# Closing an expert's first token group after four batches, and sending list entries one at a time

## The chip, the core and the metric

The kernel runs on one core of a Trainium2 chip. A core has five engines that run side by side: PE (TensorE, matmuls and transposes), DVE (VectorE), ACT (ScalarE), POOL (GpSimd) and SP (SyncE, which here only issues DMAs). They wait for each other through semaphores; each runs its own instructions strictly in order. The metric is the device time of one execution in microseconds (us), lower is better.

## The reference

```python
def reference(...):                        # B=8 batches, H=8 heads, 512 local + 32 global rows, D=64
    s_g  = scale * q_g @ concat(k_g, k_l).T            # global rows see everything
    out_g = softmax(s_g) @ concat(v_g, v_l)
    s_l  = concat(scale * q_l @ k_g.T, banded(scale * q_l @ k_l.T))   # |i - j| <= 32
    out_l = softmax(s_l) @ concat(v_g, v_l)
    x = rows of concat(out_g, out_l): 8 * 544 = 4352 tokens, 512 features
    do_compute = x @ w_skip > 0                        # tokens that go through an expert
    e_idx = argmax(x @ w_gate); gate_w = softmax(x @ w_gate)[e_idx]
    out = x;  out[do] += gate_w * (relu(x[do] @ w1[e_idx]) @ w2[e_idx])   # 8 experts, F = 1024
```

## The kernel before

**Attention** runs in 32 *units*, one for each pair of heads of a batch (`u` is the unit, `b = u // 4` the batch). The loop body is a list of step names, `ORDER`, which is walked once per unit; `cur`, `prev` and `old` are the pairs of units u, u-1 and u-2, so two more turns of the loop (u = 32 and 33, with `NU` = 32) drain the pipeline. Every engine gets its instructions in the order in which these steps issue them. Steps of weight here: `probs` (DVE, ACT: masked scores and exponentials), `scale 0` and `scale 1` (POOL, L435, multiply by the inverse sums), `scale_g` (POOL, L468), `turn` (PE, L476, transposes of the scaled probabilities), `turn_pg` (PE, L492), `turned` (DVE and ACT, L483, copies out of PSUM), `values` (PE, L530/L539), `leave` (ACT and DVE, L560). `rows` and `late_rows` turn a finished batch back to rows and write them to `out`.

**Routing.** When a batch's (or a pair of batches') rows are done, `route` returns some twenty small steps that find each token's expert and its place in that expert's list. They go into the list `stages`; each `seam` in `ORDER` (seven per unit) calls `tick`, which pops one (two from u = 28 on). `counts` (PE, L644 to L650) sums over tokens and needs `ohb` from DVE or POOL. The result `slu` holds list addresses, and one `send` per 128 tokens then writes (token, weight) entries into the DRAM list `lst` with an indirect DMA from POOL (L688). Batches go in the groups (0,1), (2,3), (4,5), 6, 7 with 8, 9, 8, 4 and 5 sends. Up to unit 28 the step `sends` issues two at the end of a unit, in units 29 and 30 up to four; in unit 30 one more goes at each of four seams, and batch 6's four go at the end of unit 31.

**First expert.** Its first group of 256 list places has to be complete before the others are. So `base[:, 0]` is raised to at least 256 after batch 5, `slots` (SP) loads the group's entries from `lst` at the end of unit 30, and in unit 31 `index` (DVE, L102) and `gather` (POOL, two indirect DMAs, L119) fetch its tokens into `xfirst`. `turn_x` (PE, L206) transposes them in turn 32.

**Experts.** Then eight experts are computed one after the other, each with a group of 256 tokens, and those with more tokens with a second group. Sends that remain (batch 7's) go out in `lists()` during the first expert, whose second group and the next expert's first one are gathered after that.

Line numbers in profile rows are those of this kernel.

## Time and profile before

| what | value |
|---|---|
| time of three runs | 475.98 us median (472.29, 475.98, 480.51) |
| the profiled execution | 477.54 us, of which 475.8 us are the span from the first to the last instruction |
| mean granted TensorE clock | 0.981 of full speed |
| PE busy | 444.5 us, 93% of the span |
| DVE, ACT, POOL busy | 302.9, 282.7 and 231.5 us |

The attention part ends and the first expert's matmuls begin at about 229 us. A row of the timeline gives start, duration, engine, line, operation and tiles; the bracket at its end is the engine's idle time just before it and who ended that.

### The profile page before, as it was taken

What the parts mean: (1) busy time and instruction counts of PE and PEld (TensorE: products, weight loads), DVE (VectorE), ACT (ScalarE), POOL (GpSimd) and SP (SyncE); (2) the same over time, 40 slices, a digit from 0 to 9 for tenths busy, and PEclk for the clock granted to TensorE, in tenths of its full rate; (3) what the DMA queues carried; (4) which work ended last, traced back from release to release, by engine and by line L of the source; (5) the groups of instructions that cost most, each with busy time, mean ns of one, the idle gap of its engine ahead of it and who ended that gap; (6) DMA issues with size and microseconds to landing.
All of it is one profiled execution on the core that took longest, in us unless ns stands there. A gap on an engine that the chain in (4) does not pass through costs nothing. (4 is left out here: it accounts for less than half of the span.)

```text
span 475.8 us, 13573 instructions
## 1 busy us (share of the span) xinstructions
PE 444.5 (93%) x4962; PEld 376.2 (79%) x4962; DVE 302.9 (64%) x1207; ACT 282.7 (59%) x867; POOL 231.5 (49%) x240
## 2 busy tenths in 40 slices
PE   7899999998899998878998999998999999999995
PEld 3677878777687777666987989997978989789894
DVE  7898888986778978573563248573823838239351
ACT  5599999998889987753432135452613636137240
POOL 7567777779866768856355032413101432004111
PEclk9799999999999999979998999999999999999999
DMA  8999898989999797401627019392820949308200
GB/s 253 288 324 314 284 326 302 299 297 234 296 269 279 191 290 228 135 2 46 201 23 286 38 50 326 118 338 70 309 102 7 302 154 318 124 21 287 79 2 34
DMA packets 50595, 93.34 MB, mean 196 GB/s; under 512 B 15644, under 2 KB 19996, under 8 KB 50496
## 3 DMA queue, kind: packets, MB, share of 16 engines
q1 hardware_dynamic: 44096, 79.73, 52.2%
q0 software_dynamic: 6400, 12.35, 7.7%
q8 instruction: 56, 0.92, 0.8%
q14 instruction: 43, 0.35, 0.3%
HBM read 82.91 MB, written 14.67 MB: 205 GB/s over the span
## 5 line engine op out<-in xcount | busy, mean ns | idle before, releaser
L398 ACT ACTIVATE prob<-prob,nmx 128x160 f32<-128x160 f32 x256 | 106.8, 424 | 17.9 <-DVE nmx L393 15.4
L435 POOL TENSOR_TENSOR prob<-prob,inv 128x640 f32<-128x640 f32 x64 | 80.7, 1262 | 37.9 <-DVE inv L431 23.6
L932 ACT ACTIVATE hh<-ph 128x256 fp32r<-128x256 f32 x72 | 27.8, 387 | 76.1 <-PE ph L926 73.7
L1014 POOL DMA_INDIRECT out_dram<-yo,six x12 | 12.2, 1019 | 118.1 <-DVE yo L1013 108.8
L945 PE MATMUL py<-w2h,hh 128*128 128x512 f32 x144 | 57.7, 401 | 1.2 <-issue 1.2
L380 PE MATMUL pss<-ks,qs 64*64 64x160 f32 x1024 | 55.4, 315 | 2.6 <-issue 1.4
L945 PE MATMUL py<-w2l,hh 128*128 128x512 f32 x144 | 56.6, 393 | 0.0
L945 PE MATMUL py<-w2h,hlw 128*128 128x512 f32 x144 | 56.5, 392 | 0.0
L539 PEld LDWEIGHTS pv<-ptT,vw 128*64 128x64 f32 x1024 | 43.1, 141 | 12.4 <-issue 11.7
L539 PE MATMUL pv<-ptT,vw 128*64 128x64 f32 (+1 forms) x1024 | 48.6, 241 | 1.9 <-issue 1.9
L398 ACT ACTIVATION_READ_ACCUMULATOR prob<-prob,nmx 128x1 f32 x256 | 49.8, 195 | 0.0
L926 PE MATMUL ph<-xh,w1l 128*128 128x256 f32 x288 | 45.4, 280 | 1.1 <-issue 1.1
L926 PE MATMUL ph<-xh,w1h 128*128 128x256 f32 x288 | 45.5, 280 | 0.7 <-PEq L1103 0.7
L380 PEld LDWEIGHTS pss<-ks,qs 64*64 64x64 f32 x1024 | 36.9, 138 | 11.1 <-issue 7.1
L926 PE MATMUL ph<-xl,w1h 128*128 128x256 f32 x288 | 45.2, 279 | 0.0
L933 DVE SCALAR_TENSOR_TENSOR hlw<-ph,hh 128x256 fp32r<-128x256 f32 x72 | 30.3, 420 | 22.6 <-ACT hh L932 20.7
L688 POOL DMA_INDIRECT lst<-dat,slu x34 | 34.1, 1004 | 14.7 <-issue 6.9
L926 PEld LDWEIGHTS ph<-xh,w1h 128*128 128x128 f32 x288 | 39.2, 189 | 1.7 <-issue 1.1
L926 PEld LDWEIGHTS ph<-xh,w1l 128*128 128x128 f32 x288 | 38.6, 188 | 1.3 <-issue 1.3
L476 PE MATMUL pst<-ident,prob 128*128 128x128 f32 x256 | 39.7, 281 | 0.0
L926 PEld LDWEIGHTS ph<-xl,w1h 128*128 128x128 f32 x288 | 38.8, 189 | 0.0
L213 ACT CAST xh<-xt 128x512 fp32r<-128x512 f32 (+1 forms) x22 | 11.2, 552 | 46.0 <-PE xt L206 46.0
(178 smaller groups left out, 970.8 us busy)
## 6 DMA issues: line engine op xcount, KB each, us to landing
raw<-in_w_dram SPq DMA_DIRECT2D x56, 512.0 KB
vw<-in_v_dram SPq DMA_DIRECT2D x32, 512.0 KB
ks<-in_kT_dram SPq DMA_DIRECT2D x32, 400.0 KB
out_dram<-xr SPq DMA_DIRECT2D x32, 256.0 KB
qs<-in_qT_dram SPq DMA_DIRECT2D x31, 256.0 KB
raw<-in_w_dram POOLq DMA_DIRECT2D x8, 512.0 KB
vgs<-in_vgl_dram SPq DMA_DIRECT2D x32, 64.0 KB
lst<-dat,slu POOLq DMA_INDIRECT x34
```

What stands on the lines that cost most here:

```text
L213: nc.scalar.copy(xh[:, c:c + step, ts_], p3[:, c:c + step])
L380: nc.tensor.matmul(banks[odd][head(h ^ odd), j * W:(j + 1) * W], q[head(h), w * QB:(w + 1) * QB], window(k[head(h)], w), start=True, stop= ...
L398: nc.scalar.activation(pt[:, i, :], pt[:, i, :], AF.Exp, bias=nmx[:, i:i + 1], scale=-1.0, accum_out=sums[:, i, 0:1],)
L435: nc.gpsimd.tensor_mul(pt[:, sl, :], pt[:, sl, :], inv[:, sl].unsqueeze(2).to_broadcast([P, 4, W]),)
L476: nc.tensor.transpose(pst[:, i * P:(i + 1) * P], pt[:, 4 * hf + i, 0:KW], ident)
L539: nc.tensor.matmul(pv[head(h), j * 96:j * 96 + n], vv[:, w, head(h)], ptT[:, w, h ^ odd, 0:n], start=False, stop=j == 3, skip_group_check= ...
L688: ins = nc.gpsimd.indirect_dma_start(out=lst, out_offset=bass.IndirectOffsetOnAxis(ap=slu[:, t:t + 1], axis=0), in_=dat[:, bs[j], t - 4 * ...
L926: nc.tensor.matmul(ph[:, 0:GRP], hl[a][:, c, f * P:(f + 1) * P], bb[:, c, :], start=i == 0, stop=i == 3 * NC - 1,)
L932: nc.scalar.activation(hh[:, f, :], ph[:, 0:GRP], AF.Relu)
L933: nc.vector.scalar_tensor_tensor(hlw[:, f, :], ph[:, 0:GRP], 0.0, hh[:, f, :].bitcast(F32), ALU.max, ALU.subtract,)
L945: nc.tensor.matmul(py, a[:, f, ts_], hl[bb][:, f, :], start=f == 0 and i == 0, stop=f == NF - 1 and i == 2,)
L1014: ins = nc.gpsimd.indirect_dma_start(out=out, out_offset=bass.IndirectOffsetOnAxis(ap=sidx, axis=0), in_=yo, in_offset=None, bounds_check= ...
```

## The change

Five things change. (1) `base[:, 0]` is raised after batch 3 (`FIRST = 4`) and not after batch 5; the first group's entries are loaded at the end of unit 27 (before: 30), and its tokens gathered in unit 29 (before: 31), from the first four batches' rows alone. (2) The address sum over eight experts is no longer made for a whole group in two DVE steps (`slot`, `slu`): the offset `do` becomes a ninth column of `pos`, and each `send` issues its own small DVE reduce into its column of `slu` just ahead of its indirect DMA. (3) From unit 29 on sends go one at a time, at the first, fourth and sixth seam of a unit; until unit 28 they still go two per unit, and those of batches 2 and 3 that remain go at the end of unit 27. (4) Batch 6's routing gets 16 empty steps (12 ahead, 4 before `counts`). (5) The forced emptying of `stages` moves from unit 31 to turn 32, that of `sends` from unit 31 to turn 33.

```diff
--- before.py
+++ after.py
@@ -626,8 +626,13 @@
                     return wk.tile([P, 9, E] if e else [P, 9], dt, name=name + "2")[:, 0:T]
                 return rt.tile([P, 5, E] if e else [P, 5], dt, name=name, bufs=2)[:, 0:T]
 
-            mx, se, do, slot = (small(n, e=False) for n in ("mx", "se", "do", "slot"))
-            ex, oh, pos = (small(n) for n in ("ex", "oh", "pos"))
+            mx, se, do = (small(n, e=False) for n in ("mx", "se", "do"))
+            ex, oh = (small(n) for n in ("ex", "oh"))
+            pos9 = (
+                wk.tile([P, 9, E + 1], F32, name="pos2") if len(bs) > 1
+                else rt.tile([P, 5, E + 1], F32, name="pos", bufs=2)
+            )[:, 0:T]
+            pos = pos9[:, :, 0:E]
             ohb = small("ohb", BF16)
             slu = small("slu", U32, e=False)
             f8 = first8.unsqueeze(1).to_broadcast([P, T, E])
@@ -668,7 +673,7 @@
                 lambda: nc.vector.tensor_tensor(oh, over(mx), f8, ALU.is_equal),
                 lambda: eng.tensor_mul(ohb, oh, over(do)),
                 lambda: nc.vector.reduce_sum(se, ex, axis=AX.X),
-                lambda: eng.tensor_scalar(do, do, -BIG, BIG, ALU.mult, ALU.add),
+                lambda: eng.tensor_scalar(pos9[:, :, E], do, -BIG, BIG, ALU.mult, ALU.add),
                 lambda: eng.tensor_scalar_add(se, se, 1.0e-9),
                 lambda: None,
                 counts,
@@ -679,12 +684,15 @@
                 lambda: nc.vector.tensor_add(base, pc[0][:, n:n + E], base),
                 lambda: eng.tensor_mul(pos, pos, ohb),
                 weight,
-                lambda: nc.vector.reduce_sum(slot, pos, axis=AX.X),
-                lambda: nc.vector.tensor_add(slu, slot, do),
             ]
+            if bs[0] == B - 2:
+                steps[12:12] = [lambda: None] * 4
+                steps[0:0] = [lambda: None] * 12
 
             def send(t):
                 j = min(t // 4, len(bs) - 1)
+                with nc.allow_low_precision(reason="sums are whole and below 2**24"):
+                    nc.vector.reduce_sum(slu[:, t:t + 1], pos9[:, t], axis=AX.X)
                 ins = nc.gpsimd.indirect_dma_start(
                     out=lst, out_offset=bass.IndirectOffsetOnAxis(ap=slu[:, t:t + 1], axis=0),
                     in_=dat[:, bs[j], t - 4 * j, :], in_offset=None,
@@ -696,6 +704,7 @@
 
         lgb, lgs, lgw, xrs = {}, {}, {}, {}
         LK = 0
+        FIRST = 4
 
         def batch_rows(b, k, halves=(0, 1)):
             T = 5 if b % 4 == 3 else 4
@@ -744,7 +753,7 @@
                     bs, lgw[bs[0]][:, 0:T], T, nc.vector if b >= B - 2 else nc.gpsimd
                 )
                 stages.extend(steps)
-                if b == B - 3:
+                if b == FIRST - 1:
                     stages.append(
                         lambda: nc.vector.tensor_scalar_max(base[:, 0:1], base[:, 0:1], float(GRP))
                     )
@@ -794,7 +803,7 @@
 
                 def seam():
                     tick(1 if u < NU - 4 else 2)
-                    if u >= NU or u == NU - 2 and next(nth) in (0, 1, 4, 5):
+                    if u > NU - 4 and next(nth) in (0, 3, 5):
                         send_some(1)
 
                 def late_rows():
@@ -825,9 +834,9 @@
                             batch_rows(bp, 4)
 
                 def first_x():
-                    if u == NU - 1:
+                    if u == NU - 3:
                         index(first, 0)
-                        gather(xfirst, six[:, 0, 0, :], (B - 2) * S)
+                        gather(xfirst, six[:, 0, 0, :], FIRST * S)
 
                 def last_x():
                     if u == NU:
@@ -862,19 +871,19 @@
                     weights[0].split(nc.gpsimd, 2)
 
                 def after():
-                    if u == NU - 2:
+                    if u == NU - 5:
                         send_some(len(sends))
                         slots(first, 0)
-                    if u == NU - 1:
+                    if u == NU:
                         tick(len(stages))
 
                 def last_sends():
-                    if u == NU - 1:
+                    if u == NU + 1:
                         send_some(len(sends))
 
                 def some_sends():
-                    if u < NU - 1:
-                        send_some(2 if u < NU - 3 else 4)
+                    if u < NU - 3:
+                        send_some(2)
 
                 loose = dict(
                     loads_g=loads_g, loads_pair=loads_pair, loads_v=loads_v,
```

The order of instructions shows what that moves. First POOL from unit 29 to the end of attention (`lst<-dat,slu` is a send, numbered `slu` is batches 4 and 5, plain `slu` is batches 6 and then 7; `prob` is a `scale`, `probg` a `scale_g`, `xfirst` the gather). Before:

```order
L688 DMA lst<-dat,slu_3667 34816x2 x4
L435 TENSOR_TENSOR prob<-prob,inv 128x640
L688 DMA lst<-dat,slu_3667 34816x2 x2
L435 TENSOR_TENSOR prob<-prob,inv 128x640
L688 DMA lst<-dat,slu_3667 34816x2 x2
L435 TENSOR_TENSOR prob<-prob,inv 128x640
L468 TENSOR_TENSOR probg<-probg,ing 128x640
L119 DMA xfirst<-out_dram,six 128x512 x2
L435 TENSOR_TENSOR prob<-prob,inv 128x640 x2
L688 DMA lst<-dat,slu 34816x2 x4
L154 DMA raw<-in_w_dram 128x1024 x2
L688 DMA lst<-dat,slu 34816x2 x5
```

and in the changed kernel, from unit 29's gather to the `scale 1` of unit 31:

```order
L119 DMA xfirst<-out_dram,six 128x512 x2
L696 DMA lst<-dat,slu_3675 34816x2
L435 TENSOR_TENSOR prob<-prob,inv 128x640
L696 DMA lst<-dat,slu_3675 34816x2
L435 TENSOR_TENSOR prob<-prob,inv 128x640
L696 DMA lst<-dat,slu_3675 34816x2 x2
L435 TENSOR_TENSOR prob<-prob,inv 128x640
L696 DMA lst<-dat,slu_3675 34816x2
L435 TENSOR_TENSOR prob<-prob,inv 128x640
L696 DMA lst<-dat,slu_3675 34816x2
L468 TENSOR_TENSOR probg<-probg,ing 128x640
L696 DMA lst<-dat,slu_3675 34816x2
```

The gather goes from unit 31 to unit 29, and the sends of batches 4 and 5, which stood as four, two and two, are spread singly or in pairs until unit 31; after the last `scale` there follow three sends, a load, the fourth send, a load and batch 7's five, where it was four sends, two loads and five.

Next PE at the end of unit 30 (`pp` is batch 6's `counts`, `pst` are transposes, `pss` the next unit's scores). Before:

```order
L539 MATMUL pv<-ptT,vw_123 64x64 x8
L476 MATMUL pst<-ident,prob 128x128 x8
L644 LDWEIGHTS tri
L644 MATMUL pp<-ohb,tri 128x32
L646 LDWEIGHTS ones
L646 MATMUL pp<-ohb,ones 128x24
L646 LDWEIGHTS ones
L646 MATMUL pp<-ohb,ones 128x16
```

and in the changed kernel the same place:

```order
L539 MATMUL pv<-ptT,vw_123 64x64 x8
L476 MATMUL pst<-ident,prob 128x128 x8
L380 MATMUL pss<-ks_144,qs_141 64x160 x8
L551 MATMUL pv<-pgT,vgs_130 64x4x32 x8
L380 MATMUL pss<-ks_144,qs_141 64x160 x8
L530 MATMUL pv<-ptT,vw_124 64x32 x2
```

Batch 6's `counts` has left the end of unit 30; it now stands in turn 32, behind the first of its `values` steps.

Last DVE at the end of unit 16, the first unit with sends (`ptT<-pst` is `turned 0`). Before:

```order
L430 TENSOR_REDUCE inv<-sumt_149 128x4
L431 RECIPROCAL inv<-inv 128x4
L483 COPY ptT<-pst 128x8x64
L511 STREAM_TRANSPOSE pgT<-prob 128x128
L393 ISA prob,nmx<-pss,m_first 128x160
```

and in the changed kernel:

```order
L430 TENSOR_REDUCE inv<-sumt_149 128x4
L431 RECIPROCAL inv<-inv 128x4
L483 COPY ptT<-pst 128x8x64
L695 TENSOR_REDUCE slu_1785<-pos_1783 128x1 x2
L511 STREAM_TRANSPOSE pgT<-prob 128x128
L393 ISA prob,nmx<-pss,m_first 128x160
```

The two reduces of the unit's two sends stand behind `turned 0`; each send on POOL now waits for its reduce.

## Rows read from the trace of the kernel before

**Rows 1.** Busy time by stretch, with granted clock (PEclk), DMA share, GB/s.
```profile
core 0: us, PE busy (x) PEld busy (x) DVE busy (x) ACT busy (x) POOL busy (x), PEclk, DMA share, GB/s
...
196.00:206.00 10.00, 6.46 (x103) 4.65 (x101) 5.58 (x32) 5.40 (x21) 6.91 (x7) 0.98 0.28 82
206.00:213.00 7.00, 6.86 (x95) 5.92 (x96) 5.43 (x36) 4.18 (x16) 4.28 (x5) 0.54 0.03 3
...
218.00:224.00 6.00, 4.17 (x60) 3.23 (x60) 1.58 (x6) 0.45 (x2) 3.80 (x4) 1.00 0.02 1
```

**Rows 2.** Timeline of PE, units 29 to 31.
```profile
199.26 0.81 PE L380 MATMUL pss<-ks,qs 64*64 64x160 f32 x15 [1.00 <-issue]
...
202.65 0.50 PE L539 MATMUL pv<-ptT,vw 128*64 128x64 f32 x9 [0.45 <-issue]
...
206.14 0.21 PE L644 MATMUL pp<-ohb,tri 128*128 128x32 bf16 x1 [1.96 <-DVE ohb L669]
```

**Rows 3.** Timeline of DVE, end of unit 30.
```profile
204.32 1.09 DVE L666 TENSOR_TENSOR oh<-oh,first 128x32 f32<-128x32 f32 x1
...
205.89 0.19 DVE L669 TENSOR_TENSOR ohb<-oh,do 128x32 bf16<-128x32 f32 x1
```

**Rows 4.** Timeline of POOL, units 29 to 32.
```profile
193.60 1.01 POOL L688 DMA_INDIRECT lst<-dat,slu  x1 [0.30 <-DVE pgT L511]
...
197.47 0.97 POOL L688 DMA_INDIRECT lst<-dat,slu  x1 [0.30 <-issue]
198.46 1.27 POOL L435 TENSOR_TENSOR prob<-prob,inv 128x640 f32<-128x640 f32 x1
...
204.12 1.25 POOL L435 TENSOR_TENSOR prob<-prob,inv 128x640 f32<-128x640 f32 x1 [1.94 <-DVE inv L431]
...
217.79 1.06 POOL L688 DMA_INDIRECT lst<-dat,slu  x1 [0.17 <-issue]
...
221.74 0.97 POOL L688 DMA_INDIRECT lst<-dat,slu  x1 [0.30 <-issue]
```

**Rows 5.** Timeline of PE, turns 32 and 33.
```profile
218.19 1.34 PE L539 MATMUL pv<-ptT,vw 128*64 128x96 f32 x32
...
223.97 0.65 PE L551 MATMUL pv<-pgT,vgs 64*64 64x128 f32 x12 [1.25 <-ACT xT L560]
```

**Rows 6.** Timeline of ACT, turn 32.
```profile
223.55 0.37 ACT L560 COPY xT<-pv 128x256 f32<-128x256 f32 x1 [5.57 <-remote]
```

**Rows 7.** Timeline of DVE, turn 32.
```profile
221.30 0.29 DVE L563 TENSOR_REDUCE xTg<-pv 128x32 f32<-128x128 f32 x1 [2.95 <-PE xt L206]
```

**Rows 8.** Timeline of POOL, units 16 and 17.
```profile
106.04 1.20 POOL L688 DMA_INDIRECT lst<-dat,slu  x1 [0.18 <-issue]
...
110.97 1.27 POOL L468 TENSOR_TENSOR probg<-probg,ing 128x640 f32<-128x640 f32 x1
```

**Rows 9.** Timeline of DVE, end of unit 16.
```profile
106.21 0.66 DVE L483 COPY ptT<-pst 128x512 f32<-128x512 f32 x1
```

**Rows 10.** Timeline of PE, `turn_pg` in units 17 and 27.
```profile
112.30 0.66 PE L492 MATMUL psgT<-ident,probg 128*128 128x128 f32 x4 [0.79 <-POOL probg L468]
...
178.15 0.66 PE L492 MATMUL psgT<-ident,probg 128*128 128x128 f32 x4
```

**Rows 11.** Timeline of POOL, units 26 and 27.
```profile
173.31 1.01 POOL L688 DMA_INDIRECT lst<-dat,slu  x1 [0.15 <-issue]
...
176.83 1.26 POOL L468 TENSOR_TENSOR probg<-probg,ing 128x640 f32<-128x640 f32 x1
```

**Rows 12.** Timeline of DVE, end of unit 26.
```profile
173.51 0.66 DVE L483 COPY ptT<-pst 128x512 f32<-128x512 f32 x1
```

**Rows 13.** The tile `slot`: duration ns min/median/max, first and last start, forms.
```profile
L682 DVE TENSOR_REDUCE slot<-pos x5: 154/212/224, 101.3 to 233.3; 128x8 f32<-128x64 f32 x2, 128x9 f32<-128x72 f32 x1, 128x4 f32<-128x32 f32 x1, 128x5 f32<-128x40 f32 x1
L683 DVE TENSOR_TENSOR slu<-slot,do x5: 157/166/1070, 102.6 to 233.5; 128x8 uint32<-128x8 f32 x2, 128x9 uint32<-128x9 f32 x1, 128x4 uint32<-128x4 f32 x1, 128x5 uint32<-128x5 f32 x1
```

**Rows 14.** The page, part 5: an expert matmul, mean ns of one.
```profile
L926 PE MATMUL ph<-xh,w1h 128*128 128x256 f32 x288 | 45.5, 280 | 0.7 <-PEq L1103 0.7
```

## The prediction

> **What bounds the kernel now.** I read the clock and the stretches first, then PE's timeline where a stretch is not full, and then whoever ends PE's waits. PE is busy for 93% of the span, so most of what this change can touch is the part that PE does not fill. The change works on the end of the attention part, from unit 29 on, and in small on the units before it that send list entries. In the stretch from 196 to 206 us PE is busy for 6.46 of 10 us. From 206 to 213 it is busy for 6.86 of 7 us, but at a granted clock of 0.54, which is the lower of its two levels, 1.2 GHz, for nearly all of it. From 218 to 224 it is busy for 4.17 of 6 us [rows 1]. What PE did before the clock fell is in its timeline: it paused 1.00 us before 199.26 and 0.45 us before 202.65, and then waited 1.96 us, until 206.14, for `ohb`, the last product that batch 6's `counts` needs [rows 2]. That chain runs on DVE, where one product that feeds it, 128x32, took 1.09 us and `ohb` itself stands at 205.89 [rows 3].
>
> The second thing to see is what POOL does in those stretches. It issues four sends in a row, the first at 193.60 and the fourth at 197.47, and unit 29's `scale 1` stands behind them at 198.46; another four go from 217.79 to 221.74 [rows 4]. In the second run ACT, which only needs PE's `values`, sits idle for 5.57 us until 223.55 [rows 6], though PE's rows say that these matmuls were issued from 218.19 on and took 1.34 us; DVE's reader of the same bank waits 2.95 us until 221.30 [rows 7]; and PE then waits 1.25 us for ACT [rows 5]. So results of PE seem to reach the others late while sends run in a row. The trace shows it twice at this end and names no cause.
>
> **The change part by part.** The sum is made against the profiled execution's own time, 477.54 us (a span of 475.8 us and 1.74 us around it); the median of the three runs, 475.98, is 1.56 us lower.
>
> First, batch 6's empty steps. Twelve ahead and four before `counts` put `ohb` into unit 31 and `counts` into turn 32, over half a unit later, so PE's 1.96 us for it go [rows 2]. At the end of unit 30 the next in line are the next unit's scores, whose keys and queries are loaded two units ahead, so nothing that I see is late there in its place. I take -2.0; the ends are 0, if `scale` or another step holds PE as long, and -2.0.
>
> Second, the slow clock. It follows that pause. If the pause goes and the clock stays up, the 6.86 us of matmuls between 206 and 213 us need 6.86 x 0.54 = 3.7 us, 3.2 less. But DVE is busy for 5.43 us of the same 7 us [rows 1], and PE can't run ahead of it by more than a unit's buffers; that leaves 7.0 - 5.43 = 1.6. The ends are 0 (the clock falls in any case) and -3.2; I take -1.6, the end that DVE sets.
>
> Third, sends singly. Unit 29's run of four is replaced by the two gathers and two sends, each on its own, and unit 31's gathers by sends, so POOL has as many indirect DMAs in units 29 to 31 as before, in shorter runs. The pauses beside the run are worth 1.00 + 0.45 us [rows 2]; the ends are 0 and -1.45, and I take half, -0.7. Against it, batch 6's sends, four in a row from 217.79, now start only after `leave` of turn 32, two in turn 32 and two in turn 33, one of these behind a weight load. One send and the gap to the next take (221.74 - 217.79) / 3 = 1.32 us [rows 4]. Turn 33 is a chain from PE to ACT and back to PE, and what is late there moves the first expert. The best end is that PE's 1.25 us go [rows 5], the worst that two more sends lie on that chain, 2 x 1.32 = +2.6. I take +0.5: as many sends run beside the drain as before, a little later.
>
> The Trainium skill, on the page "SBUF — State Buffer", section "SBUF: two separate sides", says that only the port pair shared by DVE and POOL is contended for, and that PE and ACT never wait on anyone. By that rule sends in a row cannot hold PE's or ACT's work up, their spreading is worth nothing, and the sum below would be 0.2 us smaller in size; the ACT row at 223.55 does not look like that rule, but it does not show whom ACT waited for.
>
> Fourth, the reduces. Ten group steps go and 34 small ones come. The old sum over eight experts took 154 to 224 ns and the old last step mostly 157 to 166, with one at 1070 [rows 13]. A reduce of one column of tokens is no larger than the smallest of these, so I take 0.15 us: 34 x 0.15 = 5.1 us come, and 5 x 0.21 + 4 x 0.16 + 1.07 = 2.8 go. On DVE itself that lies in idle time (it is busy for 302.9 of 475.8 us). The wait that it adds is POOL's: a send now stands behind the reduce, and the reduce behind `turned 0`. In unit 16 `turned 0` runs from 106.21 for 0.66 us [rows 9], so the first send can start at 106.21 + 0.66 + 0.15 = 107.0, where it started at 106.04 [rows 8]: 1.0 us later. Queued behind it on POOL are the second send, `scale 1`, and the next unit's `scale_g` at 110.97, and for that one PE's `turn_pg` waits already, 0.79 us before 112.30 [rows 10]. So PE waits 1.0 us longer there. In unit 26 it is the same: `turned 0` from 173.51 [rows 12], reduce done at 174.3, first send at 173.31 [rows 11]; `scale_g` ends at 176.83 + 1.26 = 178.09 and `turn_pg` starts at 178.15 [rows 10], so again 1.0 us. Where the next unit has no `scale_g` the `scale 1` has most of a unit to spare. In all +2.0 if nothing absorbs it. Unit 27 sends three, so its `scale 1` is later by the 1.0 and another 1.32 us, which is the high end: +2.0 + 1.3 = +3.3. The low end is 0. I take +1.5, near the sum of the two rows.
>
> Fifth, what costs nothing. The tokens gathered two units sooner: PE takes `xfirst` in turn 32 without a wait in front of it in the timeline, so an earlier arrival has nobody to serve; what it does is to trade places with sends on POOL. The list load at the end of unit 27 puts SP behind the last send's landing, ahead of the loads for unit 30, which are wanted more than a unit later. Closing the group sooner changes no amount of work: by the reference's inputs the first four batches already hold 288 tokens of the first expert, the first six 303, both over 256, and the total is 395 either way, so the same branches are taken; the page's 288 expert matmuls of one kind are nine passes of 32, eight first groups and one full second one [rows 14]. The first expert's own wait for the lists begins with batch 7's sends, which are as many and as late as before.
>
> The sum: -2.0 - 1.6 - 0.7 + 0.5 + 1.5 = -2.3 us, which is 475.2 for the profiled execution, and 475.98 - 2.3 = 473.7 for a median.
>
> **The rivals.** *All of it works.* The pause, the slow clock, the pauses beside the runs and PE's wait in the drain go, and the reduces cost nothing: -2.0 - 3.2 - 1.45 - 1.25 = -7.9, or 468.1. For it speaks that the slow clock has a clear pause before it; against it that DVE and POOL are busy for most of those units, too. Chance 0.2.
>
> *The slow clock moves.* PE still pauses somewhere between 196 and 224 us, as there is idle time of PE in both ends of this stretch [rows 1], and the clock falls there instead. Then -2.0 - 0.7 + 0.5 + 1.5 = -0.7 is left, about 475.3: no difference. Chance 0.25.
>
> *Slower: sends held by DVE.* POOL is in order, and 34 sends now each wait for a reduce of their own in DVE's queue. The price is the +3.3 of the early units and the +2.6 of the drain with no gain but the pause: -2.0 + 3.3 + 2.6 = +3.9, and +5.9 if PE waits for `scale` in place of `ohb`: 479.9 to 481.9. It decides from the point where the time by which a send is later, 1.0 us here, exceeds what `scale 1` and `scale_g` have to spare, which in units 16 and 26 is nothing. For it speaks `turn_pg`'s row at 112.30, against it that units 17 and 27 are two of 32. Chance 0.15.
>
> The SBUF page of the Trainium skill, in the same section, also says that a DVE operation with two SBUF inputs and a POOL operation that reads SBUF lock each other out for the whole instruction. The trace agrees: the 1.09 us product on DVE started at 204.32, while POOL's `scale` ran from 204.12 for 1.25 us, and ended 0.04 us after it [rows 3, 4]. By that rule 0.9 of the 1.96 us (1.09 against the 0.19 of a product of the same size, `ohb`) are luck of the place, and one-input reduces would not be held.
>
> **How the numbers follow.** My forecast of -2.3 has 0.4, and what is between it and the rivals is theirs as above. The predicted time is 473.7. The low end reaches the first rival and 1 us beyond it, since medians spread too (three runs lay between 472.29 and 480.51): 467.0. The high end takes the third rival's lower figure: 480.0. A difference of 2% is 9.5 us, about what a measurement of this kernel can tell from no change. No sum of bounds reaches it, so only noise or a stretch that I priced wrongly would: faster by over 2% 0.07, within 2% 0.87, slower by over 2% 0.06.
>
> **What would show it.** Right: no wait of PE for `ohb` at the end of unit 30; a granted clock near 1.00 in what is now 206 to 213 us; `turn_pg` of units 17 and 27 about 1 us later behind `scale_g`; the first expert's matmuls 2 to 4 us earlier than at 229 us. Wrong: the clock falls in turns 32 and 33 or at the first expert's start; PE idle more than 2 us between 218 and 224 us with sends beside it; a wait of PE for `xfirst`, which would mean that the gather was nearer to its deadline than it looks.

## The result and the profile after

The changed kernel takes 478.96 us (median of 20 runs, 477.27 to 482.52), the kernel before beside it 473.90 us (20 runs, 469.97 to 480.51). The ratio is 1.0118, 95% interval 1.0093 to 1.0142: slower by about 5.6 us, where -2.3 us were forecast. The time itself lies in the range, which was 467.0 to 480.0; the sign is wrong. The profiled execution after took 478.45 us (a span of 476.7 us); the one before, 477.54, lies in the upper part of the runs of before. So the two traces differ by only 0.9 us: they show where waits came and went, not the whole of the loss.

First the stretches, as in [rows 1], with two longer ones beside them and a part of the second, and then these two in the kernel before:

```profile
206.00:213.00 7.00, 5.18 (x95) 3.95 (x93) 6.89 (x32) 3.95 (x15) 4.91 (x5) 1.00 0.03 3
204.00:216.00 12.00, 8.24 (x133) 6.21 (x130) 10.64 (x49) 7.50 (x31) 7.61 (x7) 0.90 0.07 13
216.00:220.00 4.00, 4.00 (x20) 4.00 (x19) 2.27 (x18) 2.50 (x10) 2.53 (x3) 0.50 0.01 0
216.00:228.00 12.00, 11.76 (x156) 10.71 (x154) 7.58 (x38) 5.74 (x16) 7.30 (x7) 0.82 0.01 2
```

```profile
204.00:216.00 12.00, 9.78 (x119) 8.45 (x117) 8.85 (x52) 7.19 (x28) 8.68 (x8) 0.72 0.12 26
216.00:228.00 12.00, 9.55 (x139) 7.85 (x140) 5.18 (x16) 4.42 (x12) 6.80 (x8) 1.00 0.09 24
```

The clock of 206 to 213 us is now 1.00, as hoped, but PE is busy for only 5.18 of the 7 us, and the low clock is not gone. The two longer stretches have 0.90 and 0.82, where they had 0.72 and 1.00, so over these 24 us the mean is 0.86 in both kernels: the low clock has moved to behind PE's new wait below (0.50, the lower of its two levels, from 216 to 220 us), and none of it is saved. PE's timeline shows the wait that took the place of the one for `ohb` [rows 2]; the first two rows answer to [rows 10], the last to [rows 5]:

```profile
111.92 0.66 PE L492 MATMUL psgT<-ident,probg 128*128 128x128 f32 x4 [1.39 <-POOL probg L468]
...
180.62 0.66 PE L492 MATMUL psgT<-ident,probg 128*128 128x128 f32 x4 [0.73 <-POOL probg L468]
...
214.94 1.11 PE L492 MATMUL psgT<-ident,probg 128*128 128x128 f32 x4 [2.83 <-POOL probg L468]
...
229.03 1.90 PE L580 MATMUL pr<-idw,xT 128*128 128x137 f32 x14 [1.28 <-ACT xT L560]
```

In unit 31 PE waits 2.83 us for `scale_g`, where at the end of unit 30 it waited 1.96 us for `ohb`. PE's wait in the drain is 1.28 us and was 1.25. POOL's timeline, for units 16, 26, 27 and 31 ([rows 8, 11, 4] of before):

```profile
105.67 1.20 POOL L696 DMA_INDIRECT lst<-dat,slu  x1 [1.39 <-DVE pgT L511]
107.17 0.98 POOL L696 DMA_INDIRECT lst<-dat,slu  x1 [0.30 <-issue]
108.16 1.28 POOL L435 TENSOR_TENSOR prob<-prob,inv 128x640 f32<-128x640 f32 x1
...
175.79 1.00 POOL L696 DMA_INDIRECT lst<-dat,slu  x1 [1.36 <-DVE slu L695]
...
183.14 1.01 POOL L696 DMA_INDIRECT lst<-dat,slu  x1 [1.36 <-DVE slu L695]
184.45 0.97 POOL L696 DMA_INDIRECT lst<-dat,slu  x1 [0.30 <-issue]
185.72 0.97 POOL L696 DMA_INDIRECT lst<-dat,slu  x1 [0.30 <-issue]
...
212.59 1.00 POOL L696 DMA_INDIRECT lst<-dat,slu  x1 [0.48 <-DVE nmx L393]
213.62 1.26 POOL L468 TENSOR_TENSOR probg<-probg,ing 128x640 f32<-128x640 f32 x1
```

Ahead of the first send of units 16, 24, 25, 26 and 27 POOL now stands idle for 1.34 to 1.47 us, and most of these sends run while the next unit's scores are on their way. The sends of units 17, 18 and 19 are hardly held (0.54 us at most). In unit 31 a late single stands directly ahead of the `scale_g` that PE waits for, but by DVE's timeline most of that wait has another cause:

```profile
210.39 1.78 DVE L669 TENSOR_TENSOR oh<-lg,mx 128x32 f32<-128x32 f32 x1
...
212.90 0.16 DVE L464 RECIPROCAL ing<-ing 128x1 f32<-128x1 f32 x1
```

`ing`, the other input of `scale_g`, is ready only at 213.06, and `scale_g` starts at 213.62, so the send can have cost 0.56 us of the 2.83 at most. Ahead of `ing` on DVE stands a product of batch 6's routing, which the empty steps moved into unit 31; it took 1.78 us (0.18 us in the trace of e1, below, as L664).

Now DVE and PE in units 16, 17, 25, 27 and 28 of the changed kernel:

```profile
105.21 0.22 DVE L695 TENSOR_REDUCE slu<-pos 128x1 uint32<-128x9 f32 x2
...
105.48 0.72 PE L380 MATMUL pss<-ks,qs 64*64 64x160 f32 x16
...
108.54 0.33 DVE L393 CUSTOM_DVE_ANT_0 prob<-pss,m_even 128x160 f32<-128x160 f32 x1 [1.66 <-PE pv L539]
...
159.97 0.72 PE L380 MATMUL pss<-ks,qs 64*64 64x160 f32 x16
...
163.05 0.33 DVE L393 CUSTOM_DVE_ANT_0 prob<-pss,m_even 128x160 f32<-128x160 f32 x1 [1.70 <-PE pv L539]
...
178.70 0.32 DVE L393 CUSTOM_DVE_ANT_0 prob<-pss,m_even 128x160 f32<-128x160 f32 x1 [1.68 <-PE pv L539]
...
187.56 0.33 DVE L393 CUSTOM_DVE_ANT_0 prob<-pss,m_even 128x160 f32<-128x160 f32 x1 [2.93 <-remote]
```

and at the same step of units 17 and 25 in the kernel before:

```profile
109.07 0.33 DVE L393 CUSTOM_DVE_ANT_0 prob<-pss,m_even 128x160 f32<-128x160 f32 x1 [0.42 <-PE pss L380]
...
162.33 0.33 DVE L393 CUSTOM_DVE_ANT_0 prob<-pss,m_even 128x160 f32<-128x160 f32 x1 [0.16 <-PE pss L380]
```

The reduces are as cheap as priced, 0.15 us each (34 take 4.0 us in all by the groups of lines, as two in a row overlap). What is new are DVE's waits of 1.66 to 2.93 us in the middle of a unit's scores, and each has sends beside it. DVE waits there for the scores of L380 (where the bracket names L539, that is only what PE finished last before DVE went on). By PE's rows these end at 106.20 in unit 17 and at 160.69 in unit 25, over 2.3 us before DVE goes on. Where the time went by unit, worked out from DVE's timeline (from the first of a unit's eight L393 score steps to that of the next; "to experts" is from unit 31 to the first expert's first matmul), in us:

```
unit            16   17   18   19   20   24   25   26   27   28   29    30   to experts
before        6.48 7.63 6.58 7.57 6.27 6.06 7.75 6.00 7.07 6.85 10.82 8.95  20.66
after         5.60 8.99 6.67 7.71 6.30 5.36 9.73 5.94 7.71 9.34  9.95 7.20  21.22
e1            5.70 7.63 6.77 7.58 6.28 6.12 7.73 5.77 7.43 7.82  9.91 8.34  20.35
```

Of the units behind held sends, 17, 25 and 28 lose 1.4, 2.0 and 2.5 us, unit 27 0.6 and unit 26 nothing; units 18, 19 and 20, behind sends that are hardly held, lose 0.14 us at most. Units 29 and 30 give 2.6 us back, unit 24 0.7 (its two-input step of 1.07 us, L683, is gone [rows 13]). One trace is a single execution: unit 16 takes 5.71 us in e5, whose edit does not touch it, and unit 27 takes 9.33 us in the changed kernel's second trace (e16); units 17 and 25 repeat there (9.00 and 9.55).

### The profile page after: what moved, and what is told of

It reads as the page before. It is cut to its first block, busy times and chain, and to the rows that moved or that the text cites. A ratio compares the mean times of both kernels' runs of the same rounds, so it can differ in the third digit from the quotient of the medians.

```text
span 476.7 us, 13617 instructions
## 1 busy us (share of the span) xinstructions
PE 441.5 (93%) x4962; PEld 373.1 (78%) x4962; DVE 304.2 (64%) x1231; ACT 282.5 (59%) x867; POOL 231.9 (49%) x240
## 4 chain that ended last, share of the span: by engine, by line
PE 31%; issue 25%; DMA 21%; DVE 8%; ACT 6%; POOL 6%; POOLq 1%; another core or an unknown queue 1%; ACTq 0%
DMA out_dram<-yo,six 19%; PE pv L539 5%; PE pss L380 5%; ACT prob L398 5%; PE pst L476 4%; PE ph L935 2%; PE pv L551 2%; PE psg L444 2%; PE pr L597 2%; DVE prob L393 2%; PE pr L580 2%; PE psgT L492 2%; POOL probg L468 1%; PE pl L606 1%; PE pv L530 1%
## 5 line engine op out<-in xcount | busy, mean ns | idle before, releaser
L539 PEld LDWEIGHTS pv<-ptT,vw 128*64 128x64 f32 x1024 | 43.0, 137 | 18.1 <-issue 16.4
L539 PE MATMUL pv<-ptT,vw 128*64 128x64 f32 (+1 forms) x1024 | 49.9, 237 | 6.5 <-issue 5.5
L380 PE MATMUL pss<-ks,qs 64*64 64x160 f32 x1024 | 53.3, 308 | 1.8 <-DMA qs<-in_qT_dram 0.9
L380 PEld LDWEIGHTS pss<-ks,qs 64*64 64x64 f32 x1024 | 36.3, 135 | 10.2 <-issue 5.2
L189 DVE TENSOR_TENSOR w2l<-raw,w2h 128x1024 fp32r<-128x1024 f32 x28 | 34.1, 1219 | 4.9 <-ACT w2h L188 4.4
```

Of the source, the lines that this page charges most:

```text
L189: eng.tensor_sub(lo, raw, hi.bitcast(F32))
L380: nc.tensor.matmul(banks[odd][head(h ^ odd), j * W:(j + 1) * W], q[head(h), w * QB:(w + 1) * QB], window(k[head(h)], w), start=True, stop= ...
L539: nc.tensor.matmul(pv[head(h), j * 96:j * 96 + n], vv[:, w, head(h)], ptT[:, w, h ^ odd, 0:n], start=False, stop=j == 3, skip_group_check= ...
```

## The experiments

Every ratio is to the kernel before in the same session. Four questions are asked in turn: which part of the change costs, what a send costs, whether it can be put elsewhere, and how far that depends on the place of the run.

**Which part: e1, the changed kernel with the address sums by group again.**

```diff
+                lambda: nc.vector.reduce_sum(slot, pos, axis=AX.X),
+                lambda: nc.vector.tensor_add(slu, slot, do),
...
-                    nc.vector.reduce_sum(slu[:, t:t + 1], pos9[:, t], axis=AX.X)
```

> The changed kernel with its one-reduce-per-send taken back: the list addresses of a group are again made in two DVE steps ahead of its sends, all else stays as changed. Theory A (the reduce behind the copy of turned 0 lets each pair of sends start about 1 us later, at the start of the next unit, and there PE's results reach DVE late) expects most of the loss back: 475 to 476 us, 0.3 to 0.5% over the kernel before, and the units that follow sends (17, 25, 28) at their old lengths of 7.6, 7.8 and 6.9 us. Theory B (the loss is in units 29 to 33, where single sends stand ahead of scale and scale_g on POOL) expects 478 to 479 us, as the changed kernel.

474.48 us, ratio 1.0082 (1.0050 to 1.0115). Units 17 and 25 are as before (table above), unit 28 is not. So about 0.4% of the 1.2% goes with the reduces (by the two intervals 0.36%, give or take 0.41), and 0.8% stays.

**e2, the kernel before with nothing but the reduces per send** (two empty steps keep the other steps in their places).

```diff
-                lambda: nc.vector.reduce_sum(slot, pos, axis=AX.X),
-                lambda: nc.vector.tensor_add(slu, slot, do),
+                lambda: None,
+                lambda: None,
...
+                    nc.vector.reduce_sum(slu[:, t:t + 1], pos9[:, t], axis=AX.X)
```

> The kernel before with only the reduces moved into the sends; two empty steps stand for the two that go, so that sends keep their places. Theory A expects 477 to 478 us (0.6 to 0.9% over the kernel before), with units 17 and 25 longer by 1 to 2 us. Theory B expects 473.5 to 474.5, no difference.

479.74 us, ratio 1.0180 (1.0139 to 1.0222): alone, the reduces cost more than the whole change. Units 17 and 25 take 9.00 and 9.50 us, as after. The largest loss beside them is unit 30, of 12.86 us where it was 8.95, as POOL's first send of unit 29 and then DVE show:

```profile
201.44 1.01 POOL L695 DMA_INDIRECT lst<-dat,slu  x1 [4.16 <-DVE slu L694]
...
207.21 0.33 DVE L393 CUSTOM_DVE_ANT_0 prob<-pss,m_even 128x160 f32<-128x160 f32 x1 [4.49 <-remote]
```

The run of four sends, which began at 193.60 before [rows 4], waits for its reduces and falls on the start of unit 30. The late singles of the change avoid this.

**e3, the kernel before with nothing but the early close** (`FIRST` of 4, the list load behind three sends at the end of unit 27, the gather in unit 29).

```diff
-                if b == B - 3:
+                if b == 3:
...
-                    if u == NU - 1:
+                    if u == NU - 3:
...
-                    if u == NU - 2:
+                    if u == NU - 5:
                         send_some(len(sends))
                         slots(first, 0)
+                    if u == NU - 2:
+                        send_some(len(sends))
```

> The kernel before with only the first expert's first group closed after four batches: list load at the end of unit 27 behind three sends, gather in unit 29 ahead of four sends, late sends and routing as before. Theory A expects 473.5 to 475 us: a third send in unit 27 costs up to 1.3 us, the gather is not waited for. Theory B expects 474 to 476, as the gather adds to what POOL has ahead of its scales in unit 29.

473.94 us, ratio 1.0045 (1.0005 to 1.0084). The third send at the end of unit 27 begins 0.5 us after the first score step of unit 28, where in the kernel before the last send of that unit began 0.8 us ahead of it, and DVE waits at the start of unit 28, 7.86 us long (6.85 before):

```profile
180.49 0.97 POOL L688 DMA_INDIRECT lst<-dat,slu  x1 [0.31 <-issue]
...
182.42 0.33 DVE L393 CUSTOM_DVE_ANT_0 prob<-pss,m_even 128x160 f32<-128x160 f32 x1 [1.14 <-PE pss L380]
```

That is 1.0 us. What else the early close costs this trace does not place: unit 30, behind the moved gathers, is 2.8 us longer than before (11.76 us), unit 29 is 1.5 and the way to the experts 2.4 us shorter.

**e4, the changed kernel with the reduces of the sends up to unit 27 issued ahead of `turned 0`** (a step `sums` behind `late_rows`; a send then finds its address made).

```diff
+                def sums():
+                    if u < NU - 3:
+                        for fn in sends[:3 if u == NU - 5 else 2]:
+                            fn(True)
```

> The changed kernel with the reduces of the sends up to unit 27 issued ahead of the copy of turned 0 in DVE's order and their DMAs where they are; single sends from unit 29 on unchanged. Theory A expects that sends start as early as in the kernel before, so units 17, 25 and 28 lose 1 us or more each and the time is 475 to 476.5 us. Theory B expects 478.5 to 479.5, no difference to the changed kernel.

474.46 us, ratio 1.0068 (1.0043 to 1.0093). It takes the gate away in part only: in unit 16 POOL still idles, 0.79 us ahead of the first send where it was 1.39, and units 17 and 25 still take 8.40 and 9.30 us in its trace, yet the time is down by as much as in e1, within the intervals. So the reduces are worth 0.4 to 0.5% (clear of noise in e4: 0.50%, give or take 0.35), and by where they stand, since e4 has all 34 of them:

```profile
105.08 1.20 POOL L702 DMA_INDIRECT lst<-dat,slu  x1 [0.79 <-DVE slu L698]
```

**e5, the kernel before with nothing but batch 6's room** (16 empty steps, and the emptying one turn and two turns later).

```diff
+            if bs[0] == B - 2:
+                steps[12:12] = [lambda: None] * 4
+                steps[0:0] = [lambda: None] * 12
```

> The kernel before with only the 16 empty steps for batch 6 and the later emptying of stages and sends. If the two terms of the prediction hold (PE's wait for ohb goes, 2.0 us, and the clock stays up, 1.6 us), 469 to 471 us against a kernel before of 472 to 474. If the slow clock or the pause only moves, as it did in the changed kernel, no difference beyond 1 us.

472.90 us, ratio 1.0004 (0.9974 to 1.0034). The wait for `ohb` is gone, and this is what PE's timeline and one stretch have in its place:

```profile
209.34 0.65 PE L492 MATMUL psgT<-ident,probg 128*128 128x128 f32 x4 [0.96 <-POOL probg L468]
...
223.51 3.54 PE L580 MATMUL pr<-idw,xT 128*128 128x137 f32 x14 [2.04 <-DVE xT L560]
```

```profile
218.00:228.00 10.00, 7.53 (x75) 6.76 (x75) 2.62 (x8) 2.63 (x8) 4.14 (x6) 0.72 0.30 37
```

PE now waits 0.96 us for `scale_g`, where it did not wait, and 2.04 us in the drain, where it waited 1.25 [rows 5]; and the low clock (mean 0.72 from 218 to 228 us, where it was 1.00) has come to the drain. As e5 has the later emptying too, a gain of the room could hide behind a cost of that; apart they were not run.

**e7, e1 with the late singles at the third, fourth and sixth seam**, so that none stands directly ahead of `scale_g` in unit 31.

```diff
-                    if u > NU - 4 and next(nth) in (0, 3, 5):
+                    if u > NU - 4 and next(nth) in (2, 3, 5):
```

> The changed kernel with group addresses as in e1_group_slu, and the late single sends at the third, fourth and sixth seam, so that in unit 31 no send stands right ahead of scale_g on POOL. If PE's wait for scale_g of unit 30 and what the clock does after it matter, 471.5 to 473 us; if not, 474 to 475 as e1_group_slu.

476.92 us, ratio 1.0081 (1.0047 to 1.0115), as e1: nothing gained. There was little to gain: in e1's own trace `scale_g` of unit 31 waits for DVE's `ing` and not for the send, and PE's wait for it is 0.33 us.

**What a send costs: e6 and e9, the changed kernel with the 17 sends of batches 0 to 3 replaced by POOL copies** behind the same reduces, 512 or 1024 elements long; **e8, the kernel before without those sends; e10, the kernel before with the long copies in their place.** In e6 and e8, too, those tokens have no list entries.

```diff
+                if bs[-1] <= 3:
+                    nc.gpsimd.tensor_copy(
+                        xfirst.rearrange("p a d -> p (a d)"),
+                        slu[:, t:t + 1].to_broadcast([P, NSUB * DM]),
+                    )
+                    return
```

> The changed kernel with the 17 sends of batches 0 to 3 replaced by POOL copies of 128x512 into the still unused xfirst, each waiting for the same reduce; the lists lack those entries, so the experts' rows of these tokens are not computed rightly, while the amount of work stays. Theory H (an indirect DMA that POOL issues holds up PE's results to the others while it runs) expects unit 17 near 7.6 us, unit 25 near 7.7 and unit 28 near 7, and 474 to 476 us. Theory Q (the sends cost by standing ahead of scale and scale_g in POOL's queue) expects them to stay near 9.0, 9.7 and 9.3, and 478 to 480 us.

> The kernel before without the 17 sends of batches 0 to 3 (their list entries are missing, the experts' work stays the same in amount). It gives what these sends cost in the attention part where they stand before the change. Theory H expects 2 to 5 us less than before, as each pair still holds PE's results for about 2 us at the end of its unit. Theory Q expects at most 1 us less, since PE waits for scale_g only 0.8 us behind them.

> The changed kernel, its 17 sends of batches 0 to 3 replaced by POOL copies of 128x1024, each gated by the same reduce; their list entries are left out. A copy takes about as long (1.3 us estimated from 0.65 us for 128x512) as a send with the gap to the next one (1.32 us), so POOL is held as long. If the sends cost by being indirect DMAs, the time stays near 465 us, as with the short copies. If they cost by the time for which they hold POOL's queue, it comes back to 474 to 479 us.

> The kernel before, its 17 sends of batches 0 to 3 replaced in their old places by the same copies of 128x1024, not gated by a reduce of their own; their list entries are left out. Indirect DMAs as the cause: near 466 us, as without those sends. POOL's queue as the cause: near 474 us, as before.

| in place of the 17 early sends | in the kernel before | in the changed kernel |
|---|---|---|
| nothing | 0.9845 (0.9802 to 0.9887), e8 | not run |
| copies of 512 | not run | 0.9841 (0.9803 to 0.9879), e6 |
| copies of 1024 | 0.9890 (0.9827 to 0.9953), e10 | 0.9971 (0.9934 to 1.0007), e9 |
| the sends | 1 | 1.0118 (1.0093 to 1.0142) |

Without them the kernel before takes 466.43 us, 7.4 less, or 0.44 us for each send, of which the forecast knew nothing: it priced only what the change moves. Two copies of 1024 take 2.14 us; two sends with the gaps around them hold POOL from 105.86 to 108.53 in before, 2.67. So the copies are somewhat too short to be quite like sends, and the last step of each column (1.1% and 1.5%) is only in part proof that a DMA costs more than its time on POOL. The pair e10 and e9 shows the gate with no early DMA in it; they are 0.8% apart (0.1 to 1.5), but e9 carries the rest of the change as well, so not all of that is the gate. First e10, then e9, POOL and PE in units 16 and 17:

```profile
105.44 2.14 POOL L689 CAST xfirst<-slu 128x1024 f32<-128x1024 uint32 x2
...
111.30 0.66 PE L492 MATMUL psgT<-ident,probg 128*128 128x128 f32 x4 [0.97 <-POOL probg L468]
```

```profile
104.88 2.14 POOL L697 CAST xfirst<-slu 128x1024 f32<-128x1024 uint32 x2 [1.15 <-DVE slu L695]
...
110.72 0.66 PE L492 MATMUL psgT<-ident,probg 128*128 128x128 f32 x4 [2.16 <-POOL probg L468]
```

POOL idles 1.15 us for the reduce, and PE waits 2.16 - 0.97 = 1.2 us longer for `scale_g`: the prediction's fourth step, in its own place, with 1.0 priced.

**Elsewhere: e11, the pairs taken apart**, one send ahead of `scale 0` and one at the unit's end; **e12, one per unit** ahead of `scale 0` in units 16 to 23.

```diff
+                    elif u < NU - 3 and n == 3:
+                        send_some(1)
...
-                        send_some(2 if u < NU - 3 else 4)
+                        send_some(1 if u < NU - 3 else 4)
```

> The kernel before, each pair of sends up to unit 28 taken apart: one ahead of scale 0 (fourth seam), one at the old place at the unit's end. If what a send costs is that results of PE come late while it runs, and two in a row exceed what the unit can spare, units 16 to 28 get shorter, 2 to 6 us in all: 468 to 472. If each send costs its 0.44 us wherever it stands, or POOL's queue sets it: 472 to 475, no difference.

> The same, but in units 16 to 23 one send per unit alone, ahead of scale 0, so the first eight reach over eight units. If only runs of two cost, units 16 to 19 come down to the 6.3 us that they take without sends, and the time is below that of the split pairs by 1 to 3 us. If each send has its own price, the two are alike.

473.27 us, ratio 1.0000 (0.9959 to 1.0040), and 473.16, 1.0024 (0.9983 to 1.0065): no gain. In e11 one send ahead of `scale 0` moves both scales, and DVE's L511 waits for the second:

```profile
112.19 1.01 POOL L688 DMA_INDIRECT lst<-dat,slu  x1 [0.16 <-DVE inv L431]
113.23 1.26 POOL L435 TENSOR_TENSOR prob<-prob,inv 128x640 f32<-128x640 f32 x1
...
114.53 0.31 DVE L511 STREAM_TRANSPOSE pgT<-prob 128x128 f32<-128x128 f32 x1 [1.76 <-POOL prob L435]
```

In the kernel before that wait was 0.46 us. One wait was traded for another.

**e13 and e14: the kernel before with the sends up to unit 28 behind `scale 1`**, as pairs, or one per unit until unit 23.

```diff
                 def last_sends():
+                    if u < NU - 3:
+                        send_some(1 if u < NU - 8 else 2)
```

> The kernel before, each pair of sends up to unit 28 behind the unit's scale 1 in place of ahead of it, so that on POOL no scale of that unit stands behind a send; the next scale or scale_g comes some 3 us later. If the early sends cost by standing in POOL's queue ahead of scale 1, most of their 7 us comes back: 467 to 469. If they cost because PE's results come late while they run, they now run beside the next unit's scores, which DVE awaits, and the time is as before or longer: 473 to 478.

> The same, with one send per unit in units 16 to 23 and two from unit 24 on. Queue as the cause: like the pairs behind scale 1 or 1 us better, 466 to 469. Late results as the cause: one send holds results up for 1 us and not for 2.5, so units 17 to 20 lose less than with pairs, and the time lies 1 to 3 us below that of the pairs behind scale 1, but not below 470.

466.59 us, ratio 1.0044 (1.0016 to 1.0071), and 464.15, 1.0002 (0.9978 to 1.0027). Neither gains on the kernel before. But that took 464.07 us beside them (29 runs, 461.51 to 467.01), 8 to 10 us less than in every session until then.

**The place of the run: e15**, e1 with the early close taken back (`FIRST` of 6, load at the end of unit 30, gather in unit 31), came in the same session.

> The changed kernel with group-wise sums and with the first group closed after batch 5, loaded at the end of unit 30 and gathered in unit 31, as before; what is left of the change is the late sends going singly, batch 6's room and the later emptying. If the early close costs the rest (it read 1.0045 alone), this is like before: a ratio of 1.000 to 1.004. If the late sends and the drain cost it: 1.006 to 1.010.

465.00 us, ratio 0.9996 (0.9968 to 1.0025). Its trace shows what is different there. First the changed kernel, then e15, at the same four instructions of unit 17 (two sends, PE's global scores, DVE's first step behind them):

```profile
114.46 1.01 POOL L696 DMA_INDIRECT lst<-dat,slu  x1 [0.17 <-issue]
115.78 0.97 POOL L696 DMA_INDIRECT lst<-dat,slu  x1 [0.30 <-issue]
...
115.68 1.03 PE L444 MATMUL psg<-ks,qgs 128*64 128x512 f32 x4
...
117.57 0.23 DVE L420 CUSTOM_DVE_ANT_1 smg<-pss,zero 128x64 f32<-128x64 f32 x1 [1.48 <-PE psg L444]
```

```profile
114.50 1.01 POOL L691 DMA_INDIRECT lst<-dat,slu  x1 [0.17 <-issue]
115.82 0.97 POOL L691 DMA_INDIRECT lst<-dat,slu  x1 [0.31 <-issue]
...
115.72 1.03 PE L444 MATMUL psg<-ks,qgs 128*64 128x512 f32 x4
...
116.05 0.22 DVE L420 CUSTOM_DVE_ANT_1 smg<-pss,zero 128x64 f32<-128x64 f32 x1
```

POOL's and PE's rows agree within 0.04 us; DVE has its operand 1.5 us sooner. What is late, in the one place and not in the other, is the event by which DVE learns that PE is done. (The ends of matmuls in a trace are modelled, so whether the product itself is late, or only the word of it, these rows can't tell.) The kernel before has this very wait too, 1.40 us ahead of 117.87, so here it is no part of the loss; at the scores of units 17 and 25, above, it is.

Counted over a whole trace, with an event late when it comes over 0.35 us behind the modelled end of its matmul, and "beside" for an indirect DMA of POOL, send or gather, that runs then or just before: 64 of 131 beside one in the trace of before and 55 of 121 in that of after, but 3 of 419 and 2 of 430 with none beside; in e13, e14 and e15 0 of 129, 2 of 134 and 0 of 134 beside one. (The counts move by a few with where "just before" ends.) So the changed kernel has no more late events than the one before; what changed is what waits for them.

PE is not untouched either. Here are the same 32 value matmuls near the start of unit 17, first in the changed kernel, with sends from 105.67 to 108.15, then in e15, with sends from 105.70 to 108.19:

```profile
106.28 1.02 PE L539 MATMUL pv<-ptT,vw 128*64 128x96 f32 x17
107.75 0.29 PE L539 MATMUL pv<-ptT,vw 128*64 128x64 f32 x2 [0.44 <-issue]
108.47 0.61 PE L539 MATMUL pv<-ptT,vw 128*64 128x64 f32 x13 [0.44 <-issue]
```

```profile
107.51 1.39 PE L539 MATMUL pv<-ptT,vw 128*64 128x96 f32 x32
```

They take 2.8 us and 1.4 us. "Issue" says that the profile shows nothing that PE waited for. Between 100 and 220 us such pauses of PE add up to 5.1 us in the trace of before (13 of them) and 6.9 us in that of after (16), nearly all of them beside an indirect DMA. Without the early sends it is 1.1 us at most (e6, e8, e9, e10), and the traces of e13, e14, e15 and e18 have none.

**e16, the changed kernel once more, and e17, e14 once more**, to be read by where they fell.

> The changed kernel, unchanged, once more. If the kernel before reads about 464 us beside it, PE's results are on time there: then late results as the cause of the loss expect a ratio of 0.997 to 1.005, and POOL's queue as the cause expects 1.010 or more, as its order is the same. If the kernel before reads 472 us or more, results are late there, and both expect 1.009 to 1.014 again.

> The kernel before with one send per unit behind scale 1 in units 16 to 23 and two from unit 24 on, once more. If the kernel before reads 472 us or more beside it, results are late there: then late results as the cause expect 0.995 to 1.003, and POOL's queue ahead of scale 1 as the cause expects 0.985 to 0.992. If the kernel before reads about 464 us, both expect 1.000 again.

The kernel before read 472.42 us, and in the two traces 64 of 121 and 59 of 125 events beside an indirect DMA were late. e16: 477.76 us, ratio 1.0115 (1.0078 to 1.0152), the result again. e17: 474.29 us, ratio 1.0026 (0.9991 to 1.0061), as late results had it and not POOL's queue. In it units 17 to 20 take 25.1 us together (28.1 in before, 24.8 in e8 without these sends), so one send behind `scale 1` is free there, but units 22 to 25 and 28, which get sends in other places than before, lose that again.

**e18, e15 once more**, for what stays of the loss in e1.

> The late singles, the room and the later emptying with the early close left out, once more. Where the kernel before reads 472 us or more: if the early close costs the rest of the loss, 0.999 to 1.004; if the late sends and the drain cost it, 1.006 to 1.010. Where it reads about 464 us, 1.000 again, and the question stays open.

465.05 us, ratio 1.0017 (0.9994 to 1.0041), but again at a place with results on time (before 463.57 us, 1 of 135 events late). What the late singles and the drain cost where results are late was not measured by itself.

## Why the prediction was wrong

By its own terms, in us, each measured ratio taken of 473.9; the parts were run in different surroundings, so they need not add up, and the last row is only what is left over:

| term | forecast | measured | from |
|---|---|---|---|
| pause and slow clock (first, second) | -3.6 | +0.2 (-1.2 to +1.6) | e5, which has the later emptying too |
| reduces (fourth) | +1.5 | +2.4 (+0.7 to +4.0) | after against e4; +1.7 against e1 (-0.2 to +3.6); alone in the kernel before +8.5, e2 |
| early close (fifth) | 0 | +2.1 (+0.2 to +4.0) | e3 |
| late singles and drain (third) | -0.2 | +0.9 (about -2 to +4) | the rest of +5.6 |

**The step that failed most** is the first with the second: that the 1.96 us for `ohb` would go with "nothing that I see is late there in its place", and the clock stay up. The wait went as said, but batch 6's routing, moved on by the empty steps, then stood on DVE ahead of `ing`, and PE waited 2.83 us for `scale_g` in unit 31, at most 0.56 of it for the send in between; and the low clock followed that wait (0.50 from 216 to 220 us; over 24 us the mean is 0.86 in both kernels). That was the rival of the moving clock, priced at 475.3, and e5 bears it out: +0.2 us where the two steps forecast -3.6. Of the signs of being right two came whole (no wait for `ohb`, a clock of 1.00 from 206 to 213 us) and one in part (`turn_pg` waits 0.6 and 0.7 us longer); the fourth failed, as the first expert's matmuls begin at 231.15 us, later than the 229 of before. Of the signs of being wrong the falling clock came.

**The fifth step failed too.** I looked at who waits for `xfirst` and found nobody, rightly. What e3's trace shows is that the early load needs the sends of batch 3 out by unit 27, so three stand in a row at its end, and unit 28 is 1.0 us longer; the rest of the 2.1 us it does not place. Only the high end of the fourth step had the third send. (The first six batches hold 306 tokens of the first expert, not 303; nothing rests on it.)

**The fourth step** had the mechanism right: the send behind the reduce, the reduce behind `turned 0`, 1.0 us later, shown in POOL's rows after, and in its effect by e9's PE row. The size, +1.5, lies inside what was measured. But in the changed kernel itself the loss does not show mainly where I put it (`turn_pg` waits 1.39 for 0.79 us in unit 17, 0.73 for none in unit 27) but in DVE's waits for PE's scores near the unit's start (1.66, 1.70, 1.68 and 2.93 us in units 17, 25, 27 and 28). That the size was near is in part luck.

**The third step** stated that results of PE seem to reach the others late while sends run, and then priced it for units 29 to 33 alone. The same holds for units 16 to 28, where the change holds the sends of five units by over 1.3 us each, most of them onto scores that DVE awaits. The slower rival named sends held by DVE and put 479.9 to 481.9 on it; in the early units that is the way it went, with late results beside its queueing.

The Trainium skill, page "SBUF — State Buffer", section "SBUF: two separate sides", says of the engines' ports that PE and ACT never wait on anyone. For the matmuls of L444 the traces agree: they take 1.03 us with sends beside them in either place. What the prediction drew from that rule, that sends in a row cannot hold PE's work up, the traces do not bear out: PE's pauses of 5.1 us in the trace of before lie nearly all beside indirect DMAs, and in that of after DVE waited 1.48 us for PE's product. Whether a port has any part in that no run here shows.

**What stays open**: what makes events late in one place and not in another; what PE waits for in its pauses; whether the changed kernel would lose at all where events are on time (it was not run there); where most of the early close's 2.1 us goes; and whether anything is left for the late singles and the drain, as the last row of the table is within noise of nothing.

## What to carry to other kernels

When a step is given a new wait, look not only at who queues behind it, but at what will run beside it at its new time. Empty steps move work and do not remove it: look at who stands behind it where it goes. Price a POOL DMA by leaving it out once: here 17 of them were worth 7.4 us, more than any place for them. And read a new time beside the kernel before on the same chip and in the same session: the place alone moved the kernel before by 8 to 10 us, and e14 by 10 (464.15 and, as e17, 474.29).

## What the runs showed of the hardware

An indirect DMA of 128 rows holds POOL for 1.0 us, with a 0.30 us gap to the next. In 16 traces of kernels, where the kernel before takes 472 to 474 us, three to five in ten of PE's completion events that have such a DMA beside them come over 0.35 us late, and DVE gets scores over 2 us behind the modelled end of their matmuls (units 17 and 25 above); in four traces, where it takes 464 us, practically none does, with sends of the same length, and between 100 and 220 us PE has no pause there of the kind above. Sessions of both kinds list the same chip number, so the chip's number is not what tells them apart; what does, no run here shows. Whether the whole 9 us between the two are late events and PE's pauses is not shown; e8, with 7.4 us for half of the sends, allows it.
